# Phase 2's first product by Strassen's algorithm in a packed attention and two-mixer kernel

## The chip, the core and the metric

One core of a Trainium2 chip runs the whole program. TensorE multiplies, VectorE and ScalarE do the element-wise work, GpSimd a few memory sets, and SyncE issues the DMAs. The metric is the device time of one launch in microseconds (us). The kernel before took 1606.13 us, the median of three runs (1604.97 to 1606.46).

## The reference, cut to what matters

```python
x = attention_twice(q, k, v, p)          # 8 x 576 x 512
x = r * ((relu(xk @ w_k) ** 2) @ w_v)    # first mixer, "phase 1"
xt = x.transpose(0, 2, 1)
u = x + (xt @ U @ V).transpose(0, 2, 1)  # rank 32, over the sequence
out = u + relu(u @ w_ch1) @ w_ch2        # 512 -> 2048 -> 512, "phase 2"
```

The change concerns `u @ w_ch1`, the first product of phase 2: 4608 tokens by 512 by 2048.

## The kernel before

Attention and the first mixer run in 12 chunks of 384 tokens, one after another; four blocks of attention lie between the first of them. This is phase 1. Its result x goes to DRAM (x2_d), summed into a 64-row product with U (psu). Phase 2 takes the same 12 chunks again.

Every fp32 number that a large matmul reads is split into two fp32r tiles, hi (a copy) and lo (the number less hi), and a product is three matmuls: hi by hi, hi by lo, lo by hi (PASS). `split` makes hi on ScalarE or VectorE and lo on VectorE.

In phase 2 a chunk goes like this. `load_u` brings x back. `h_block` adds the U-V term, two matmuls of 512 columns into a bank called psh. `t_block` transposes u by four matmuls (pst) and splits the transpose into ut. For each of the 16 blocks m of 128 hidden units, `c1_block` accumulates 12 matmuls with w_ch1's block as the weights and 384 tokens as the moving columns, and forms the hidden block: relu on ScalarE is hi, and one VectorE operation is lo. `c2_block` then runs 9 matmuls of 512 columns with hid as weights and w_ch2 as moving operand, into three banks that stay open over all 16 blocks. Both products write banks that the profile names psc. `fin` adds u and sends the rows out. All of w_ch1 and w_ch2 is split once, in the first chunk of phase 2, and stays in SBUF.

The order of instructions is a planner's. Operations are written down in program order with the tiles that they read and write; `emit` (a list scheduler) walks simulated time and gives each engine the ready operation of the lowest class, on TensorE and SyncE then the earliest in program order, on the others the one that has been ready longest. It carries its own costs, and the engines run the order that results. Lower classes go first; the casts of phase 2's weights have class 3 and fall into gaps of phase 1. A tile of a pool is granted again only when all users of the one that it replaces are done, and tiles of one tag are granted in program order. All DMAs are issued by SyncE (L311).

PSUM has eight banks: three hold the second products (ps_v), two the first products (ps_k), one psu, two the rest (ps_a).

Of the kernel before, what the change touches and what calls it, by code (L numbers as in the profile page):

```python
# [100 lines left out]
class Plan:  # L101
# [202 lines left out]
            return self.size(o) + 100.0  # L304
        return self.add((eng,), fn, (), (out,))

    def dma(self, out, in_, cls=None, after=()):
        def fn():
            o = out.get() if isinstance(out, Ref) else out
            i = in_.get() if isinstance(in_, Ref) else in_  # L310
            self.nc.sync.dma_start(out=o, in_=i)  # L311
            runs = []
            for ap in (o, i):
                n, dims = 4, list(ap.ap)
                while dims and dims[-1][0] * 4 == n:
# [3 lines left out]
        return self.add(("sp",), fn, [in_] if isinstance(in_, Ref) else [],  # L319
                        [out] if isinstance(out, Ref) else [], cls=cls, after=after)  # L320


    LAT = {"pe": {"act": 197.0, "dve": 197.0, "pool": 224.0},
# [9 lines left out]
    def emit(self):  # L333
# [67 lines left out]
        while True:  # L401
# [46 lines left out]
            if e == "sp":  # L448
# [21 lines left out]
def packed_attention_moe_mixer_kernel(  # L470
# [20 lines left out]
    P = 128  # L491
# [29 lines left out]
    def dtile(name, shape, parts=(0,)):  # L521
        return plan.fixed(dram.tile(shape, F32, name=name), parts)
# [3 lines left out]
    xu_d = [dtile(f"xu_d{b}", [P, DM]) for b in range(NBP)]  # L526
    v_d = dtile("v_d", [NP, S])
    w1_d = [dtile(f"w1_d{m}", [P, NJ * P]) for m in range(MC)]
    w2_d = [dtile(f"w2_d{m}", [P, DM]) for m in range(MC)]

    def ctile(name, shape, dt=F32):
# [377 lines left out]
    for j in range(NJ):  # L909
        cast_rows(wk[j][0], w_k[j * P:(j + 1) * P, 0:512])  # L910

    es_c = ExitStack()
    hid_p, kk_p, r_p, x2_p, xs_p = cpools = [Pool(bufs=n) for n in (2, 3, 3, 3, 1)]

    def open_c():
        es_st.close()
        w1b.obj = open_pool(es_c, "w1b", 1, "left")
        for n, pl in zip("hid kk r x2 xs".split(), cpools):
            pl.obj = open_pool(es_c, n, pl.bufs, "left")

# [132 lines left out]
    order.append(("v", MK - 2))  # L1053


    es_2r, es_2l = ExitStack(), ExitStack()
    vx_p, st_p, w2r_p, ur_p, utr_p = rpools = [Pool(bufs=n) for n in (1, 3, 1, 1, 1)]
    NR = 2

    def open_r():  # L1060
        es_att.close()
        for n, pl in zip("vx st2 w2r ur utr".split(), rpools):
            pl.obj = open_pool(es_2r, n, pl.bufs, "right")

    w2l_p, ul_p, utl_p, h_p, o_p, stl_p = lpools = [Pool(bufs=n) for n in (1, 1, 1, 3, 2, 2)]

    def open_l():
        es_c.close()
        es_x.close()
        es_w1.close()  # L1070
        for n, pl in zip("w2l ul utl h o stl".split(), lpools):
            pl.obj = open_pool(es_2l, n, pl.bufs, "left")

    w2, u_t, ut_t, xt, hh = {}, {}, {}, {}, {}
    vst_ = []

    def make_v():
        vst = plan.tile(vx_p, [P, 2, NI, 2, 64], F32R, "vst", parts=(0, 1))
        vst_.append(vst)
        for c in range(2):  # L1080
# [3 lines left out]
            for i0, i1 in ((0, 5), (5, NI)):  # L1084
# [7 lines left out]
                sl = slice(c * 32, (c + 1) * 32)  # L1092
                split(vst.at(0)[:, 0, i0:i1, :, sl], vst.at(1)[:, 1, i0:i1, :, sl], sv)

    def load_w2(m):
        pl = w2r_p if m < NR else w2l_p
        a = plan.tile(pl, [P, 2, NJ, P], F32R, f"w1_{m}", parts=(0, 1))
        b = plan.tile(pl, [P, 2, DM], F32R, f"w2_{m}", parts=(0, 1))
        sa = plan.tile(st_p, [P, 512], F32, "s", name="s_2")
        plan.dma(sa[:, 0:512], w1_d[m])  # L1100
        split(half(a, 0), half(a, 1), sa[:, 0:512].rearrange("p (j c) -> p j c", j=NJ))
        sb = plan.tile(st_p if m < NR else stl_p, [P, 512], F32, "s", name="s_2")
        plan.dma(sb[:, 0:512], w2_d[m])
        split(half(b, 0), half(b, 1), sb[:, 0:512])
        w2[m] = (a, b)

    def load_xu(b):
        xa = plan.tile(st_p, [P, 512], F32, "s", parts=(0, 1), name="xa")
# [7 lines left out]
        plan.tt(X[64:128, :], xa[64:128, 0:512], X[64:128, :], sub)  # L1116
        xt[b] = X

    def load_u(n):
        b, c = chunks[n]  # L1120
        pl = (ur_p, ul_p)[n % 2]
        t = plan.tile(pl, [P, 3, DM], F32, "u", parts=(0, 1, 2))
        for i in range(3):
            ii = 3 * c + i
            plan.dma(t.at(i)[:, i, :], x2_d[b].at(ii)[:, ii * DM:(ii + 1) * DM])
        u_t[n] = t

    def h_block(n, t):
        b, c = chunks[n]
        if t == 0:  # L1130
            ut_t[n] = plan.tile((utr_p, utl_p)[n % 2], [P, 2, NJ, CW], F32R, "ut", parts=(0, 1))
        ps = plan.bank(ps_a, "psh")
        for a in range(2):
            plan.mm(ps, vst_[0].at(a)[:, a, 3 * c + t].rearrange("p b c -> p (b c)"), xt[b],
                    start=(a == 0), stop=(a == 1))
        u = u_t[n].at(t)[:, t, :]
        plan.tt(u, ps, u, add)

    def t_block(n, t):
        ps = plan.bank(ps_a, "pst")  # L1140
        for j in range(NJ):
            plan.transpose(ps[:, j * P:(j + 1) * P], u_t[n].at(t)[:, t, j * P:(j + 1) * P], ident)
        pv = ps.rearrange("p (j c) -> p j c", j=NJ)
        sl = slice(t * P, (t + 1) * P)
        ut = ut_t[n]
# [3 lines left out]
    def c1_block(n, m):  # L1149
        ps = plan.bank(ps_k, "psc1")  # L1150
        ut, w = ut_t[n], w2[m][0]
        i = 0
        for j in range(NJ):
# [3 lines left out]
        t = plan.tile(h_p, [P, 2, CW], F32R, "h", parts=(0, 1), name="hid")  # L1157
        plan.act(half(t, 0), ps[:, 0:CW], AF.Relu)
        plan.stt(half(t, 1), ps[:, 0:CW], 0.0, half(t, 0), ALU.max, sub)
        hh[n, m] = t  # L1160

    def c2_block(n, m):
        if m == 0:
            vps[:] = [plan.bank(ps_v, "psc2") for _ in range(3)]
        h, w = hh.pop((n, m)), w2[m][1]
        for t in range(3):
            for i, (a, wi) in enumerate(PASS):
                plan.mm(vps[t], half(h, a)[:, t * P:(t + 1) * P], half(w, wi),
                        start=(m == 0 and i == 0), stop=(m == MC - 1 and i == 2))

    def fin(n, t):
        b, c = chunks[n]
        o = plan.tile(o_p, [P, 512], F32, "o")
        plan.tt(o, vps[t], u_t[n].at(t)[:, t, :], add)
        dst = out[2 * b:2 * b + 2].rearrange("b (p i) f -> (b p) i f", i=NI)
        plan.dma(dst[:, 3 * c + t, :], o)

    casts = []
    for c in range(2):
# [22 lines left out]
    for n in range(len(chunks)):  # L1202
# [15 lines left out]
            load_x(n + 1)  # L1218
        for kind, m in order:
            if kind == "k":  # L1220
                if n + 1 == len(chunks) and m >= 1 and prep0:
# [18 lines left out]
        if b == NBP - 1 and c == 1:  # L1240
            make_v()
            for m in range(NR):
                load_w2(m)
            load_xu(0)
            load_u(0)
            prep0 = [f for t in range(3) for f in (lambda t=t: h_block(0, t), lambda t=t: t_block(0, t))]
    for t, x2 in enumerate(finish(len(chunks) - 1)):
        xu_block(len(chunks) - 1, t, x2)
    plan.open(lpools, cpools + xpools + [w1a, w1b], open_l, after=[opened_r])


    for n in range(len(chunks)):
        prep = []
        if n + 1 < len(chunks):
            b1, c1 = chunks[n + 1]
            load_u(n + 1)
            prep = [("h", 0), ("h", 1), ("t", 0), ("h", 2), ("t", 1), ("t", 2)]
            if c1 == 0:
                prep = [("x", b1)] + prep
        for m in range(MC + 2):  # L1260
            if m < MC:
                if m not in w2:
                    load_w2(m)
                c1_block(n, m)
            if m >= 2:
                c2_block(n, m - 2)
            if m >= 6 and prep:
                kind, a = prep.pop(0)
                if kind == "x":
                    load_xu(a)  # L1270
                elif kind == "h":
                    h_block(n + 1, a)
                else:
                    t_block(n + 1, a)
        for t in range(3):
            fin(n, t)
    plan.emit()
    es_2l.close()
    es_2r.close()


# [29 lines left out]
```

## Time and profile before

| What | us |
|---|---|
| median of three runs | 1606.13 |
| the profiled execution | 1604.61 |
| its span, first to last instruction | 1602.8 |
| TensorE busy in it | 1545.7 |
| VectorE busy | 762.7 |
| ScalarE busy | 599.0 |
| GpSimd busy | 3.1 |

A span of 1602.8 us lies 1.8 us inside the execution's time. Busy times of TensorE are those of pipelined instructions with modelled ends, so the mean time of one matmul in the profile is longer than the distance from one to the next; the distance is read from the starts in the timeline. TensorE's weight loads (PEld) lie beside its matmuls.

### The profile page before, as it was taken

The page shows a single profiled execution, that of the slowest core. Times are in us where ns is not written, and L with a number is a line of the kernel's source. Part 1 is how long each engine was busy: PE and PEld are TensorE (multiplying, and loading weights), DVE is VectorE, ACT ScalarE, POOL GpSimd, SP SyncE. Part 2 cuts the span into 40 slices and gives each one's busy share as a digit, 9 for nine tenths or more (in the row PEclk, how much of TensorE's full clock was granted, in tenths as well). Part 3 has the DMA queues.
Part 4 walks back from the last instruction along what each step waited for, and adds up shares of the span by engine and source line. Part 5 has one row for each costly group of instructions (what it writes and reads, how often), then busy time and mean ns, then how long its engine had stood idle before and what let it go on. Part 6 is the DMA issues. An engine that isn't in the chain of part 4 may idle for free.

```text
span 1602.8 us, 20779 instructions
## 1 busy us (share of the span) xinstructions
PE 1545.7 (96%) x8116; PEld 1348.5 (84%) x8116; DVE 762.7 (48%) x1627; ACT 599.0 (37%) x1293; POOL 3.1 (0%) x18
## 2 busy tenths in 40 slices
PE   6678799999999999999999999999999999999998
PEld 5557578888888888888899999899999989999997
DVE  4898868888887786443732221222122222221211
ACT  4676566676766665454421111111111111111110
POOL 0000000000000000000000000000000000000000
PEclk9888999999999999999999999999999999999999
DMA  9966446457634334100611101011010101101000
GB/s 186 226 171 160 119 111 172 122 166 195 157 120 140 138 123 128 53 3 18 212 39 33 40 1 40 1 47 40 1 40 1 40 1 40 40 1 40 0 21 20
DMA packets 146082, 128.51 MB, mean 80 GB/s; under 512 B 92736, under 2 KB 111488, under 8 KB 145984
## 3 DMA queue, kind: packets, MB, share of 16 engines
q1 hardware_dynamic: 145984, 127.18, 28.1%
q8 instruction: 64, 1.05, 0.3%
q14 instruction: 34, 0.28, 0.1%
HBM read 89.33 MB, written 37.82 MB: 79 GB/s over the span
## 4 chain that ended last, share of the span: by engine, by line
PE 91%; DMA 2%; ACT 2%; SPq 2%; DVE 2%; issue 0%; ACTq 0%; DVEq 0%
PE psc L197 50%; PE psv L197 12%; PE psk L197 12%; PE psr L197 6%; PE psat L197 4%; PE psat L208 2%; SPq L311 2%; PE psu L197 1%; PE psh L197 1%; PE pst L208 1%; ACT a L229 1%; DMA st<-in_moe_w_v_dram 1%; DMA st<-in_moe_w_k_dram 1%; DMA qin<-in_q_dram 0%; DVE m L250 0%
## 5 line engine op out<-in xcount | busy, mean ns | idle before, releaser
L197 PE MATMUL psc<-ut,w 128*128 128x384 f32 x2304 | 433.6, 337 | 0.0
L197 PE MATMUL psc<-w,hid 128*128 128x512 f32 x1728 | 426.1, 393 | 1.1 <-ACT hid L229 1.1
L197 PEld LDWEIGHTS psc<-ut,w 128*128 128x128 f32 x2304 | 405.5, 188 | 11.7
L197 PEld LDWEIGHTS psc<-w,hid 128*128 128x128 f32 x1728 | 321.7, 188 | 61.1 <-ACT hid L229 1.5
L265 DVE SCALAR_TENSOR_TENSOR hid<-psc,hid 128x384 fp32r<-128x384 f32 x192 | 107.1, 558 | 466.9 <-ACT hid L229 466.8
L229 ACT ACTIVATE hid<-psc 128x384 fp32r<-128x384 f32 x192 | 94.3, 492 | 610.7 <-PE psc L197 610.7
L197 PE MATMUL psk<-xk,wk 128*128 128x384 f32 x1152 | 232.3, 343 | 0.5 <-DVE xk L250 0.4
L197 PE MATMUL psv<-wv,kk 128*128 128x512 f32 x864 | 227.4, 401 | 4.0 <-ACT wv L280 2.9
L197 PEld LDWEIGHTS psk<-xk,wk 128*128 128x128 f32 x1152 | 202.0, 189 | 12.6 <-issue 3.9
L197 PEld LDWEIGHTS psv<-wv,kk 128*128 128x128 f32 x864 | 159.2, 189 | 37.5 <-ACT wv L280 3.8
L197 PE MATMUL psr<-wr,xr 128*128 128x512 f32 x432 | 114.7, 408 | 3.4 <-ACT xr L280 3.4
L197 PEld LDWEIGHTS psr<-wr,xr 128*128 128x128 f32 x432 | 81.0, 194 | 23.7 <-ACT xr L280 4.1
L250 DVE TENSOR_TENSOR kk<-sq,kk 128x384 fp32r<-128x384 f32 x96 | 52.7, 554 | 60.8 <-ACT kk L280 60.4
L229 ACT ACTIVATE sq<-psk 128x384 f32<-128x384 f32 x96 | 46.7, 489 | 83.9 <-PE psk L197 83.4
L229 ACT ACTIVATE m<-x,om_t 128x384 f32<-128x384 f32 x96 | 57.6, 611 | 10.8 <-DVE xk L250 5.8
L262 DVE SCALAR_TENSOR_TENSOR m<-x,mu_t,m 128x384 f32<-128x384 f32 x96 | 57.9, 612 | 1.7 <-ACT m L229 1.5
L250 DVE TENSOR_TENSOR ut<-pst,ut 128x512 fp32r<-128x512 f32 x36 | 24.9, 692 | 68.3 <-ACT ut L229 68.3
L250 DVE TENSOR_TENSOR u<-psh,u 128x512 f32<-128x512 f32 x36 | 24.9, 692 | 49.5 <-PE psh L197 48.4
L229 ACT ACTIVATE ut<-pst 128x512 fp32r<-128x512 f32 x36 | 21.5, 599 | 67.9 <-PE pst L208 67.9
L250 DVE TENSOR_TENSOR o<-psc,u 128x512 f32<-128x512 f32 x36 | 24.6, 688 | 46.1 <-PE psc L197 44.7
L280 ACT ACTIVATE kk<-sq 128x384 fp32r<-128x384 f32 x86 | 44.7, 522 | 3.0 <-DVE sq L296 1.0
L229 ACT ACTIVATE a<-st 128x512 f32<-128x512 f32 (+2 forms) x55 | 35.6, 657 | 19.2 <-DMA st<-in_moe_w_ch_dram 4.7
(125 smaller groups left out, 1361.2 us busy)
## 6 DMA issues: line engine op xcount, KB each, us to landing
st<-in_moe_w_ch_dram SPq DMA_DIRECT2D x32, 512.0 KB, 4.4
qin<-in_q_dram SPq DMA_DIRECT2D x32, 288.0 KB, 5.5
x_d<-xo SPq DMA_DIRECT2D x16, 576.0 KB, 3.4
x_d<-x SPq DMA_DIRECT2D x36, 256.0 KB, 2.9
u<-x_d SPq DMA_DIRECT2D x36, 256.0 KB, 3.4
out_dram<-o SPq DMA_DIRECT2D x36, 256.0 KB, 2.0
kin<-in_k_dram SPq DMA_DIRECT2D x32, 256.0 KB, 5.8
vin<-in_v_dram SPq DMA_DIRECT2D x32, 256.0 KB, 5.1
```

The source lines that it names most:

```text
L197: self.nc.tensor.matmul(o, l, r, start=start, stop=stop, **k)
L208: self.nc.tensor.transpose(out.get(), in_.get(), ident.get())
L229: self.nc.scalar.activation(o, in_.get(), func, **k)
L250: return self.elem(engs, lambda e, o, x, y: e.tensor_tensor(out=o, in0=x, in1=y, op=op), out, [a, b], self.TT, cls)
L262: ("dve",), lambda e, o, x, y, z: e.scalar_tensor_tensor(out=o, in0=x, scalar=z, in1=y, op0=op0, op1=op1), out, [a, b, s], {"dve": (1.042, ...
L265: ("dve",), lambda e, o, x, y: e.scalar_tensor_tensor(out=o, in0=x, scalar=s, in1=y, op0=op0, op1=op1), out, [a, b], self.TT, cls)
L280: self.nc.scalar.activation(o, i, AF.Copy)
L311: self.nc.sync.dma_start(out=o, in_=i)
```

## The change

Phase 2 takes 9 groups of 512 tokens instead of 12 chunks of 384. For each pair of hidden blocks (f, 8 of them) the 512 x 256 weights and the 512 tokens are cut in two by two blocks: 256 of the model dimension by 128 hidden units, and 256 by 256 tokens. The four results of 128 x 256 come from seven block products with combined operands (the Winograd form of Strassen's algorithm), where eight would be the plain way. A block product is 2 x 3 matmuls of 128x128 weights and 256 columns.

The combined weights are formed by VectorE in the last two chunks of phase 1 (`make_ws`, class 3), split, and written to DRAM by SyncE; in phase 2 each block product loads its own 256 KB again (`load_ws`), issued by GpSimd's queue into one of 12 tiles. The combined tokens (`operands`) are formed for the next group behind the seventh of the eight steps of the one before. Three banks a, b and c collect the products; ScalarE and VectorE read them between products to form the shared sums. The second product's matmuls are the same, in another order; three of its four parts of a step run in the next step (`late`). Its results now take four banks, the first product three, and h_block and t_block share one.

```diff
-    def dma(self, out, in_, cls=None, after=()):
+    def dma(self, out, in_, cls=None, after=(), eng="sp"):
-            self.nc.sync.dma_start(out=o, in_=i)
+            (self.nc.sync if eng == "sp" else self.nc.gpsimd).dma_start(out=o, in_=i)
-                clock[e] = t + 60.0
+                clock[e] = t + (60.0 if e == "sp" else 1000.0)
...
+    vx_p, st_p, u_p, wb_p = rpools = [Pool(bufs=n) for n in (1, 5, 9, 12)]
...
+    def make_ws(f):
+        r = []
+        for m in (2 * f, 2 * f + 1):
+            t = plan.tile(st_p, [P, 512], F32, "s", name="raw_1")
+            plan.dma(t, w1_d[m])
+            r.append(t)
+        a11, a12, a21, a22 = [t[:, h * 256:(h + 1) * 256] for t in r for h in range(2)]
+        bl = [plan.tile(wb_p, [P, 2, 256], F32R, "wb", parts=(0, 1)) for _ in range(7)]
...
+        plan.tt(s1, a21, a22, add)
+        plan.tt(s2, s1, a11, sub)
+        plan.tt(s3, a11, a21, sub)
+        plan.tt(s4, a12, s2, sub)
+        for i, src in enumerate((a11, s2, s1, a12, s3, s4, a22)):
+            split(half(bl[i], 0), half(bl[i], 1), src)
+        for i in range(7):
+            plan.dma(ws_d[f].at(i)[:, i * 512:(i + 1) * 512], bl[i].rearrange("p a c -> p (a c)").bitcast(F32))
+
+    def load_ws(f, i):
+        t = plan.tile(wb_p, [P, 2, 256], F32R, "wb", parts=(0, 1))
+        plan.dma(t.rearrange("p a c -> p (a c)"), ws_d[f].at(i)[:, i * 512:(i + 1) * 512], eng="pool")
+        return t
...
-        plan.act(ut.at(0)[:, 0, :, sl], pv, AF.Copy)
-        plan.tt(ut.at(1)[:, 1, :, sl], pv, ut.at(0)[:, 0, :, sl], sub)
+        plan.copy(ut_[q].at((t // 2, 2 + t // 2))[:, :, t * P:(t + 1) * P], ps.rearrange("p (j c) -> p j c", j=NJ))
+
+    def operands(q):
...
+        t1, t2 = [kc(plan.tile(st_p, [P, 512], F32, "s", name="sums")) for _ in range(2)]
+        o11 = whole(b11)
+        plan.tt(t1, b12, b11, sub)
+        plan.tt(t2, b22, t1, sub)
+        plan.tt(b11, b21, t2, sub)
+        plan.tt(b12, b22, b12, sub)
+        ops[q] = [o11] + [whole(x) for x in (t2, t1, b21, b12, b22, b11)]
+
+    def product(q, f, i, name, fresh):
+        if fresh:
+            bank_abc[name] = plan.bank(ps_c1, "psc1")
+        ps = bank_abc[name][:, 0:256]
+        w, x = load_ws(f, i), ops[q][i]
+        n = 0
+        for k in range(2):
             for wi, a in PASS:
-                plan.mm(ps[:, 0:CW], w.at(wi)[:, wi, j, :], ut.at(a)[:, a, j, :], start=(i == 0), stop=(i == 11))
-                i += 1
+                plan.mm(ps, half(w, wi)[:, k * P:(k + 1) * P],
+                        half(x, a)[:, k * 256:(k + 1) * 256],
+                        start=(fresh and n == 0), stop=(n == 5), skip_group_check=True)
+                n += 1
+        return ps
...
+            a = product(q, f, 0, "a", True)
+            p1 = tmp_tile()
+            plan.copy(p1, a, ("act",))
+            b = product(q, f, 1, "b", True)
+            s = tmp_tile()
+            plan.tt(s, p1, b, add)
+            if late:
+                late.pop("22")()
+            c = product(q, f, 2, "c", True)
+            p5 = tmp_tile()
+            plan.copy(p5, c, ("act",))
+            if late:
+                late.pop("21")()
+            product(q, f, 3, "a", False)
+            h11 = hidden(a)
+            if late:
+                late.pop("12")()
+            product(q, f, 4, "b", False)
+            x22 = tmp_tile()
+            plan.tt(x22, p1, b, add)
+            plan.tt(x22, x22, p5, add)
+            h22 = hidden(x22)
+            product(q, f, 5, "c", False)
+            plan.tt(s, s, c, add)
+            h12 = hidden(s)
+            c2_block(q, 2 * f, 0, h11, False)
+            product(q, f, 6, "b", False)
+            plan.tt(p1, p1, b, add)
+            h21 = hidden(p1)
+            end = f == NF - 1
+            late = {"22": lambda q=q, f=f, h=h22: c2_block(q, 2 * f + 1, 1, h, False),
+                    "21": lambda q=q, f=f, h=h21, end=end: c2_block(q, 2 * f + 1, 0, h, end),
+                    "12": lambda q=q, f=f, h=h12, end=end: c2_block(q, 2 * f, 1, h, end)}
```

## Rows read from the trace of the kernel before

**Rows 1.** Windows: the stretch, its length; busy us and instructions by engine; clock, DMA, GB/s

```profile
600.00:763.50 163.50, 163.50 (x808) 145.71 (x807) 80.51 (x160) 79.35 (x155) 0.71 (x2) 1.00 0.15 50
763.50:1597.50 834.00, 832.89 (x4237) 753.45 (x4235) 202.51 (x340) 129.66 (x252) 0.00 (x0) 1.00 0.10 32
...
763.50:803.50 40.00, 38.93 (x200) 35.32 (x199) 28.65 (x51) 17.16 (x32) 0.00 (x0) 1.00 0.69 218
```

**Rows 2.** The chain that ended last, by engine and by line

```profile
PE 91%; DMA 2%; ACT 2%; SPq 2%; DVE 2%; issue 0%; ACTq 0%; DVEq 0%
PE psc L197 50%; PE psv L197 12%; PE psk L197 12%; PE psr L197 6%; PE psat L197 4%; PE psat L208 2%; SPq L311 2%; PE psu L197 1%; PE psh L197 1%; PE pst L208 1%; ACT a L229 1%; DMA st<-in_moe_w_v_dram 1%; DMA st<-in_moe_w_k_dram 1%; DMA qin<-in_q_dram 0%; DVE m L250 0%
```

**Rows 3.** Groups by line and form, phase 2: busy us, mean ns, idle before

```profile
L197 PE MATMUL psc<-ut,w 128*128 128x384 f32 x2304 | 433.6, 337 | 0.0
L197 PE MATMUL psc<-w,hid 128*128 128x512 f32 x1728 | 426.1, 393 | 1.1 <-ACT hid L229 1.1
L197 PEld LDWEIGHTS psc<-ut,w 128*128 128x128 f32 x2303 | 405.3, 188 | 11.7
...
L265 DVE SCALAR_TENSOR_TENSOR hid<-psc,hid 128x384 fp32r<-128x384 f32 x192 | 107.1, 558 | 466.9 <-ACT hid L229 466.8
L229 ACT ACTIVATE hid<-psc 128x384 fp32r<-128x384 f32 x192 | 94.3, 492 | 610.7 <-PE psc L197 610.7
```

**Rows 4.** Timeline of TensorE in one step of phase 2: start, us, what

```profile
1004.39 0.62 PE L197 MATMUL psh<-X,vst 128*128 128x512 f32 x2
1004.85 2.27 PE L197 MATMUL psc<-ut,w 128*128 128x384 f32 x12
1006.95 2.24 PE L197 MATMUL psc<-w,hid 128*128 128x512 f32 x9
1009.03 0.60 PE L208 MATMUL pst<-ident,u 128*128 128x128 f32 x4
1009.39 2.33 PE L197 MATMUL psc<-ut,w 128*128 128x384 f32 x12
```

**Rows 5.** Timelines of TensorE at matmuls of 256 columns, and of a weight load

```profile
346.15 0.38 PE L197 MATMUL psat<-th,ppz 64*128 64x256 f32 x1
346.37 0.28 PE L197 MATMUL psat<-tl,ppz 64*128 64x256 f32 x1
346.49 0.27 PE L197 MATMUL psat<-th,ppz 64*128 64x256 f32 x1
...
346.26 0.19 PEld L197 LDWEIGHTS psat<-tl,ppz 64*128 64x128 f32 x1
```

**Rows 6.** SyncE's DMAs at the seam; the same loads to landing; first and last

```profile
772.66 19.12 SPq L311 DMA_DIRECT2D s<-w_d  x19
...
s<-w_d SPq DMA_DIRECT2D x32, 256.0 KB, 3.1
...
L311 SPq DMA_DIRECT2D w_d<-m x32: 319/327/1530, 248.8 to 595.2; - x32
```

**Rows 7.** Groups by line and form: the nearest to the new operations

```profile
L280 ACT ACTIVATE xo<-psat 128x256 f32<-128x256 f32 x22 | 7.8, 386 | 8.4 <-PE psat L197 8.4
...
L250 DVE TENSOR_TENSOR vst<-s_v,vst 128x256 fp32r<-128x256 f32 x2 | 0.8, 422 | 0.0
...
L250 DVE TENSOR_TENSOR m<-m,a 128x512 f32<-128x512 f32 x52 | 35.1, 683 | 0.1
...
L280 ACT ACTIVATE w<-s 128x512 fp32r<-128x512 f32 x23 | 14.4, 630 | 11.3 <-DMA s<-w_d 11.1
L283 DVE CAST w<-s 128x512 fp32r<-128x512 f32 x9 | 3.6, 423 | 1.7 <-DMA s<-w_d 1.7
```

**Rows 8.** Timeline of TensorE at the seam: start, us, what, idle before

```profile
771.26 1.42 PE L197 MATMUL psc<-w,hid 128*128 128x512 f32 x5 [1.07 <-ACT hid L229]
```

**Rows 9.** Timeline of the tail

```profile
1596.14 1.37 DVE L250 TENSOR_TENSOR o<-psc,u 128x512 f32<-128x512 f32 x2 [3.72 <-PE psc L197]
...
1599.01 0.69 DVE L250 TENSOR_TENSOR o<-psc,u 128x512 f32<-128x512 f32 x1 [1.49 <-DMA out_dram<-o]
```

More of the change, by code (lines that the diff above doesn't have):

```diff
@@ L1117, in load_xu @@
         xt[b] = X
[L1119 to L1129, printed above, removed]
-        if t == 0:
[L1131 to L1137, printed above, removed]
@@ L1162, in c2_block, with load_u @@
[L1162 to L1166, printed above, removed]
-            for i, (a, wi) in enumerate(PASS):
[L1168 to L1176, printed above, removed]
+    def load_u(T):
+        b, i = divmod(T, NI)
+        u_t[T] = plan.tile(u_p, [P, DM], F32, "u")
+        plan.dma(u_t[T], x2_d[b].at(i)[:, i * DM:(i + 1) * DM])
@@ new lines, in packed_attention_moe_mixer_kernel, with h_block, t_block @@
+    prep_banks = [ps_a]
+    def h_block(T):
+        b, i = divmod(T, NI)
+        ps = plan.bank(prep_banks[0], "psh")
+        for a in range(2):
+            plan.mm(ps, vst_[0].at(a)[:, a, i].rearrange("p b c -> p (b c)"), xt[b], start=(a == 0), stop=(a == 1))
+        plan.tt(u_t[T], ps, u_t[T], add)
+    def t_block(T):
+        q, t = divmod(T, 4)
+        if t == 0:
+            ut_[q] = plan.tile(xin_p, [P, NJ, 4 * P], F32, "x", parts=(0, 1, 2, 3), name="ut")
+        ps = plan.bank(prep_banks[0], "pst")
+        for j in range(NJ):
+            plan.transpose(ps[:, j * P:(j + 1) * P], u_t[T][:, j * P:(j + 1) * P], ident)
+        plan.copy(ut_[q].at((t // 2, 2 + t // 2))[:, :, t * P:(t + 1) * P], ps.rearrange("p (j c) -> p j c", j=NJ))
@@ new lines, in hidden, with c2_block @@
+    def hidden(src):
+        t = plan.tile(mix_p, [P, 2, CW], F32R, "mx", parts=(0, 1), name="hid")
+        hi, lo = [half(t, i)[:, 0:256] for i in range(2)]
+        plan.act(hi, src, AF.Relu)
+        plan.stt(lo, src, 0.0, hi, ALU.max, sub)
+        return t
+    def c2_block(q, m, th, h, last):
+        if (q, th) not in first:
+            first.add((q, th))
+            acc[q, th] = [plan.bank(ps_c2, "psc2") for _ in range(2)]
+            fresh = True
+        else:
+            fresh = False
+        w = w2[m]
+        for t in range(2):
+            for i, (a, wi) in enumerate(PASS):
+                plan.mm(acc[q, th][t], half(h, a)[:, t * P:(t + 1) * P], half(w, wi),
+                        start=(fresh and i == 0), stop=(last and i == 2))
+        if last:
+            for t in range(2):
+                T = 4 * q + 2 * th + t
+                b, i = divmod(T, NI)
+                u = u_t.pop(T)
+                plan.tt(u, acc[q, th][t], u, add)
+                dst = out[2 * b:2 * b + 2].rearrange("b (p i) f -> (b p) i f", i=NI)
+                plan.dma(dst[:, i, :], u)
@@ L1239, in packed_attention_moe_mixer_kernel @@
                 opened_r = plan.open(rpools, A0.pools + cv.pools, open_r)
-        if b == NBP - 1 and c == 1:
-            make_v()
-            for m in range(NR):
+        if n > NCAST:
+            plan.cls = 3
+            for f in range(NF // 2):
+                make_ws((n - NCAST - 1) * (NF // 2) + f)
+            plan.cls = 1
+        if n == NCAST + 1:
+            make_v()
+            load_xu(0)
+            for T in range(4):
+                load_u(T)
+            prep0 = [f for T in range(4) for f in (lambda T=T: h_block(T), lambda T=T: t_block(T))]
@@ L1243, in packed_attention_moe_mixer_kernel @@
+        if n == NCAST + 2:
+            operands(0)
+            for m in range(2):
                 load_w2(m)
-            load_xu(0)
-            load_u(0)
-            prep0 = [f for t in range(3) for f in (lambda t=t: h_block(0, t), lambda t=t: t_block(0, t))]
     for t, x2 in enumerate(finish(len(chunks) - 1)):
         xu_block(len(chunks) - 1, t, x2)
-    plan.open(lpools, cpools + xpools + [w1a, w1b], open_l, after=[opened_r])
-    for n in range(len(chunks)):
-        prep = []
[L1254 to L1276, printed above, removed]
@@ new lines, in packed_attention_moe_mixer_kernel @@
+    plan.open(lpools, cpools, open_l, after=[opened_r])
+    ps_c2, ps_c1 = banks[0:3] + banks[5:6], banks[3:5] + banks[6:7]
+    prep_banks[0] = banks[7:8]
+    late = {}
+    for q in range(NQ):
+        prep = []
+        if q + 1 < NQ:
+            T0 = 4 * q + 4
+            for T in range(T0, T0 + 4):
+                load_u(T)
+            hs = [[lambda T=T: h_block(T)] for T in range(T0, T0 + 4)]
+            for T in range(T0, T0 + 4):
+                if T % NI == 0:
+                    hs[T - T0].insert(0, lambda T=T: load_xu(T // NI))
+            ts_ = [[lambda T=T: t_block(T)] for T in range(T0, T0 + 4)]
+            prep = [[], hs[0], hs[1] + ts_[0], hs[2] + ts_[1], hs[3] + ts_[2], ts_[3], [lambda q=q: operands(q + 1)]]
+        for f in range(NF):
+            if q == 0:
+                for m in (2 * f + 2, 2 * f + 3):
+                    if m < MC:
+                        load_w2(m)
+            a = product(q, f, 0, "a", True)
[31 more added lines that the diff above has]
+                    "12": lambda q=q, f=f, h=h12, end=end: c2_block(q, 2 * f, 1, h, end)}
+            if prep:
+                for g in prep.pop(0):
+                    g()
@@ L1277, in packed_attention_moe_mixer_kernel @@
+    for x in ("22", "21", "12"):
+        late.pop(x)()
     plan.emit()
```

84 lines of the change are left out of this document (47 added, 37 removed).

## The prediction

> **What bounds the kernel now.** I read the stages first [rows 1]. Phase 2, the stretch that the change rewrites, is 763.5 to 1597.5 us, 834 us long, and TensorE is busy in 832.9 of them at a granted clock of 1.00, its 2.4 GHz level. VectorE has work in 202.5 us of it, ScalarE in 129.7, GpSimd in none, and the DMA engines 10%. The chain of waits says the same: 91% of it is TensorE, and half of the span is the two products of phase 2, both under the name psc [rows 2]. So phase 2 is as long as its matmuls, if nothing else gets in. The means of the groups [rows 3] are latencies of overlapping instructions and no pitch; the pitch comes from the starts in the timeline [rows 4]. Twelve matmuls of the first product begin at 1004.85 and the next group at 1006.95: 2.10 us, 0.175 us each. Nine of the second product take 2.08 us, 0.231 each; a pair of U-V matmuls (psh) 0.46, four transposes (pst) 0.36. With the counts of rows 3, 192 x (2.10 + 2.08) + 33 x (0.46 + 0.36) = 829.6 us, which leaves 4.4 for the seam and small change: the pitches carry the stage.
>
> **The change: matmuls.** The first product goes from 2304 matmuls of 384 columns to 9 groups x 8 steps x 7 block products x 6 = 3024 of 256 columns: 7/8 of the columns, but 720 more instructions, each with its own weight load. The second product keeps 72 x 24 = 1728 matmuls of 512, and there are again 36 psh pairs and 36 transpose groups. All hangs on the pitch at 256 columns. The two pitches of rows 4 lie on a line of 0.4375 ns a column with 7 ns over; at 256 it gives 0.119 us. The trace has such a row nearly: fp32r matmuls of 256 columns, weights of 64 rows, each with a load of its own, start 0.12 us apart [rows 5]. I take 0.119. The ends: 0.112 if only the columns counted (256 x 0.4375 ns); and 0.188, the length of a weight load's record, if loads did not overlap [rows 3]. Against the latter, in rows 5 a load of 0.19 us begins 0.11 after the matmul before it, and the matmul that needs it 0.11 later, before the record ends.
> Before: 2304 x 0.175 = 403.2 us. After: 3024 x 0.119 = 359.9. The term is -43.3 us (-64.5 at 0.112; +165 at 0.188; it is zero at 0.133).
> A rule of the Trainium skill stands against the trace here. TensorE: Matmul & The Clock Gate, section Back-to-back issue gap, gives N/2.4 + 2.5 ns at full clock. By it 256 columns cost 109 ns and the 3024 cost an estimated 330 us, 73 us less than what the trace has for the old ones. But the same rule gives 162.5 and 216 ns where rows 4 have 175 and 231; the measurement decides.
>
> **Loads of the combined weights.** GpSimd's queue now issues 9 x 8 x 7 = 504 loads of 256 KB. TensorE's time of phase 2 after the change is about 359.9 + 1728 x 0.231 + 33 x 0.82 = 786 us, so one load is due every 1.56 us; they cost nothing if they come at that pace, since 12 tiles let the queue run some 19 us ahead and nothing else is queued on GpSimd there (its busy time in the stretch is zero [rows 1]). The trace has no transfer of this queue and none that goes from fp32 into an fp32r tile, so its pace is bounded: below, SyncE's queue issued 19 loads of the same size and 2 KB rows in 19.12 us at the seam, 1.01 us a load [rows 6]; above, if a load began only when the one before had landed, 3.1 us [rows 6]. The break-even, where loads alone fill the old 834 us, is 1.65. I take the lower end, as it is a sustained rate of this very size, and cost the loads at nothing. Were the cover gone, 0.1 us over 1.56 costs 50 us in all. Outputs and u loads add 18.9 MB, some 24 GB/s to the stream's 168; 40 us at the seam moved 218 [rows 1].
>
> **VectorE and ScalarE.** A step (two hidden blocks, 512 tokens) runs 42 x 0.119 + 24 x 0.231 = 10.5 us on TensorE. It has 6 ScalarE operations on 128x256 (two copies, four relus), 0.386 us by the nearest row, and 9 on VectorE, 0.422 [rows 7]: 2.3 and 3.8 us. That is more than today (192 x (0.49 + 0.56) [rows 3] over the phase), but under 40% of a step. What can bite is the chain inside it, since three banks are written twice or thrice. With a product at 0.71 and a half of the second product at 1.39: product 3 ends 5.6 into the step, relu, subtraction and three hand-overs of some 0.2 give the hidden block at 7.0, and its user starts at 8.4. Product 4 ends at 7.7, VectorE has read its bank by 8.5, and product 6 wants it at 9.8. Each slack is 1.3 us or more, three VectorE operations long. I cost it at nothing.
> Once a group, the 7 operands of the next are formed in the last step: 4 + 7 operations of 0.68 on VectorE and 7 copies of 0.63 on ScalarE or 0.42 on VectorE [rows 7], 7.5 us more in 10.5 that hold 3.8 already, plus what is left of adds and copies. Only three of ten tiles are free early; the rest wait for the old group's last products. The first products of the next group need the first operands only. I give each of the 8 seams 0.4 us, 3 in all.
>
> **Before phase 2.** The combined weights are formed during the last two chunks: 8 x (4 + 7) VectorE operations of 0.422 [rows 7] = 37 us, 56 copies of 0.39 on ScalarE, and the first operands, 7.5. From 600 to 763.5 us VectorE is free for 83 us and ScalarE for 84 [rows 1]; the last of the DRAM weights that they read was written at 595.2 and can be read from there on [rows 6]. TensorE is busy in all of that stretch, and the new work has the lowest class, so it goes into gaps. On SyncE's queue 56 writes (256 KB, 14.7 MB) come in front of what follows, beside the 50 GB/s of that stretch; the 14 first-product loads and splits that stood after 763.5 go away. What is late next is the seam itself: the last transpose of the first group now stands in the last k block, some 8 us ahead of phase 2, and product 1 needs two subtractions and a split after it. Today the seam has one wait of 1.07 us [rows 8]; I take 3 more.
>
> **Tail.** Today the last addition waits 1.49 us for an output buffer and comes after the two before it [rows 9]; now two additions are made in place, and the end has bubbles of a few tenths in its last hidden block. Zero in sum.
>
> **Sum.** -43.3 + 3 + 3 = -37 us. The profiled execution took 1604.6 us (span 1602.8); the median of the runs is 1.5 above. 1604.6 - 37 is 1567.3, and 1568 or 1569 on the median's footing; I say 1568.
>
> **Rivals.**
> *A. The loads set the pace.* Place: GpSimd's queue, with TensorE waiting at the weight load of each block product. It decides from 1.56 us a load, and the kernel is slower than before from 1.65. At 2.05, midway between the two ends of rows 6, the loads alone last 1033 us and the kernel ends near 763.5 + 1033 + 8 = 1805. For it: no row shows this queue, and a 256 KB load is short next to its 3.1 us of landing, so it needs two in flight at all times. Against: 12 tiles, an idle engine, and SyncE's 1.01. The Trainium skill, DMA: Bandwidth & Descriptors, section Bandwidth, has for loads issued by GpSimd 0.95 us at 64 KB and 6.15 at 1 MB; a straight line between these is an estimated 1.99 us at 256 KB, and 504 of them would end the kernel near 1775. SyncE's 1.01 for the same bytes speaks against it, no run yet shows it for GpSimd.
> *B. Waits inside the steps eat the gain.* Banks a, b and c are read by ScalarE and VectorE between products; if VectorE is late by 1.9 us somewhere in each step, past the 1.3 of slack, 0.6 x 72 = 43 us are gone and the time is about 1605; a step that loses 1 us makes it 1635. For it: adds, operands and outputs share VectorE with the chain, and each is 0.68 long. Against: under half of VectorE is used, and TensorE's order can move on to the next product.
> *C. Weight loads don't hide under 256 columns.* Decides at 0.133 us; at 0.188, 1604.6 + 165 + 6 = 1776. Rows 5 speak against it, with 64 rows of weights though, not 128.
>
> **Chances.** The forecast 0.67, A 0.15, B 0.14, C 0.04. The forecast's own range is 1540 (0.112 a matmul, no waits) to 1595 (0.125, 15 us of waits). The range goes on to 1640, over B and the near edge of A. A change under 0.2%, 3 us, can't be told from none. Faster: the forecast and 0.05 of A and B at their mild ends, 0.72; within 0.2%: 0.05, from B; slower: 0.23.
>
> **What would show it.** Right: a phase 2 near 795 us with TensorE busy throughout, groups of six 256-column matmuls every 0.71 us, idle time before them under 1%. A would show as gaps before the weight loads, released by a DMA, and loads from GpSimd more than 1.6 us apart; B as gaps released by VectorE or ScalarE; C as groups of six over 0.8 us with no gap between groups. A seam past 770 us would show that the combined weights came late.

## The result, and the profile after

The changed kernel takes 1570.7 us (median of 4 runs, 1566.98 to 1570.89), the kernel before 1605.7 on the same chip: ratio 0.9777, 95% interval 0.976 to 0.9794. The prediction was 1568, in a range of 1540 to 1640. The profiled execution took 1570.7 us with a span of 1568.9, 33.9 less than the 1602.8 of before.

The stages first, as in [rows 1]: windows of the change, with length, busy us and instructions by engine (PE, PEld, DVE, ACT, POOL), clock, DMA share, GB/s.

```profile
600.00:764.00 164.00, 164.00 (x815) 146.47 (x815) 114.60 (x265) 99.77 (x211) 8.56 (x16) 1.00 0.57 190
764.00:1563.50 799.50, 795.21 (x4959) 715.89 (x4958) 377.24 (x843) 217.99 (x529) 259.77 (x492) 1.00 0.70 189
763.50:779.50 16.00, 13.00 (x71) 9.97 (x69) 13.23 (x24) 7.74 (x15) 3.17 (x6) 1.00 0.96 301
779.50:786.50 7.00, 5.71 (x24) 5.21 (x25) 5.83 (x12) 3.22 (x7) 1.05 (x2) 0.51 0.43 134
786.50:1563.50 777.00, 777.00 (x4868) 701.13 (x4867) 358.68 (x810) 207.52 (x508) 255.56 (x484) 1.00 0.70 187
```

Phase 2 went from 834 us [rows 1] to about 800. From 786.5 us on TensorE is busy in 777.00 of 777.00 us at the 2.4 GHz level, while the DMA engines are busy in 70% of the time. All that phase 2 waits for lies in its first 23 us: 16.00 - 13.00 and 7.00 - 5.71 make 4.29 us of idle, where [rows 8] have one wait of 1.07; and in the second of these windows the granted clock is 0.51, the 1.2 GHz level, after TensorE had stood in several gaps. Before phase 2 VectorE took on 34 us and ScalarE 20 more than in [rows 1] (80.51, 79.35), and TensorE stayed busy throughout.

The groups of phase 2 in the changed kernel, as in [rows 3]: busy us, mean ns of one, idle before and what ended it.

```profile
L197 PE MATMUL psc<-w,hid 128*128 128x512 f32 x1728 | 445.9, 393 | 0.0
L197 PEld LDWEIGHTS psc<-ob,wb 128*128 128x128 f32 x3024 | 407.9, 191 | 26.4
L197 PE MATMUL psc<-ob,wb 128*128 128x256 f32 x3024 | 421.0, 284 | 0.0
L311 POOL DMA_DIRECT2D wb<-ws_d x504 | 266.4, 529 | 610.6 <-PE psc L197 513.1
L250 DVE TENSOR_TENSOR tmp<-tmp,psc 128x256 f32<-128x256 f32 x288 | 120.7, 419 | 151.3 <-PE psc L197 142.4
L229 ACT ACTIVATE hid<-tmp 128x256 fp32r<-128x256 f32 x216 | 85.2, 417 | 255.6 <-DVE tmp L250 255.5
L280 ACT ACTIVATE tmp<-psc 128x256 f32<-128x256 f32 x144 | 54.5, 379 | 136.0 <-PE psc L197 136.0
```

The matmul of 256 columns records 284 ns, but that is its latency; the price is in the starts. The steady part of phase 2, timeline of TensorE: start, us, what.

```profile
1202.59 1.55 PE L197 MATMUL psc<-w,hid 128*128 128x512 f32 x6
1203.98 0.88 PE L197 MATMUL psc<-ob,wb 128*128 128x256 f32 x6
1204.69 1.55 PE L197 MATMUL psc<-w,hid 128*128 128x512 f32 x6
1206.08 0.88 PE L197 MATMUL psc<-ob,wb 128*128 128x256 f32 x6
1206.79 1.55 PE L197 MATMUL psc<-w,hid 128*128 128x512 f32 x6
1208.18 1.59 PE L197 MATMUL psc<-ob,wb 128*128 128x256 f32 x12
```

Six of 256 columns take 0.71 us (1204.69 - 1203.98), the number that the prediction asked to see, and six of 512 take 1.39, as it reckoned for half of a second product. The rows of the GpSimd queue say the rest. In the groups above its 610.6 us of idle end with a matmul (513.1 of them): it waits until TensorE frees a tile. The waits from 790 to 1560 us (engine, line, waited for: us, times, longest us) say so too:

```profile
POOL wb L311 <- PE psc L197: 467.0, 326, 4.2
```

The loads are ahead: in that window no wait of TensorE or of its weight loads ends with a DMA. In the DMA view their median way to landing is 3.1 us, and the queues' packets hold the engines as follows (packets, MB, share of 16 engines' span):

```profile
q0 software_dynamic: 72576, 132.15, 32.4%
q1 hardware_dynamic: 154048, 141.87, 31.2%
...
wb<-ws_d POOLq DMA_DIRECT2D x504, 256.0 KB, 3.1
```

**The account.** For each matmul I took the distance from its start to the next start and summed these by kind, so that waits count with the matmul ahead of them. "Prep" is psu, psh and pst, the U-V products and the transposes that prepare a group; "rest" is all before and between, "end" what follows the last matmul's start. The experiments stand below the two kernels.

```
us                first   second   prep    rest    end     span
before            405.9   398.4    50.9    741.9   5.7     1602.8
the change        364.2   398.9    57.1    743.8   5.0     1568.9
the change again  364.1   398.9    56.6    743.4   5.0     1568.0
e1_eighth         415.7   398.9    57.3    745.1   5.0     1622.0
e2_two_loads      532.5   505.5    69.5    744.9   4.8     1857.1
e3_no_stream      364.0   399.3    55.8    744.9   5.0     1568.9
e4_sync_queue     364.2   399.0    59.0    741.8   4.5     1568.6
e5_hold3          365.5   399.5    59.0    745.5   4.4     1573.8
e6_hold6          386.9   402.0    59.5    740.7   4.4     1593.5
e7_late_w2        364.8   398.9    54.4    744.3   5.0     1567.4
e8_low_w2         364.5   399.2    54.8    745.7   5.0     1569.2
e9_few_tiles      366.6   417.5    63.8    742.2   4.7     1594.8
e10_paced_w2      363.7   399.3    54.4    744.4   5.0     1566.9
e12_two_sync      373.4   403.7    56.3    743.4   4.3     1580.9
```

The 33.9 us are -41.7 (first product), +0.5 (second), +6.2 (prep, 5.7 of it at the seam into phase 2), +1.9 (rest) and -0.7 (end). The first product has a share in the seam too: its matmuls in the first two steps of phase 2 take 132.5 and 145.8 ns from start to start, those of every later step 118.7 to 121.2, and that makes 1.7 us. "Rest" goes from 740.7 to 745.7 over kernels that run nearly the same code there, so its +1.9 is scatter of single executions.

### The profile page after: what moved, and what is told of

It reads as the page before. It is cut to its first block, busy times and chain, and to the rows that moved or that the text cites. A ratio compares the mean times of both kernels' runs of the same rounds, so it can differ in the third digit from the quotient of the medians.

```text
span 1568.9 us, 24697 instructions
## 1 busy us (share of the span) xinstructions
PE 1511.3 (96%) x8836; PEld 1313.2 (84%) x8836; DVE 971.1 (62%) x2231; ACT 706.4 (45%) x1623; POOL 270.2 (17%) x522
## 3 DMA queue, kind: packets, MB, share of 16 engines
q1 hardware_dynamic: 154048, 141.87, 31.2%
## 4 chain that ended last, share of the span: by engine, by line
PE 90%; DMA 3%; DVE 3%; ACT 2%; SPq 1%; issue 0%; DVEq 0%; ACTq 0%
PE psc L197 48%; PE psv L197 12%; PE psk L197 12%; PE psr L197 6%; PE psat L197 5%; PE psat L208 3%; SPq L311 1%; PE psh L197 1%; PE psu L197 1%; PE pst L208 1%; DMA st<-in_moe_w_k_dram 1%; DMA st<-in_moe_w_v_dram 1%; ACT a L229 1%; DMA qin<-in_q_dram 1%; DVE m L250 0%
## 5 line engine op out<-in xcount | busy, mean ns | idle before, releaser
L197 PE MATMUL psc<-w,hid 128*128 128x512 f32 x1728 | 445.9, 393 | 0.0
L197 PEld LDWEIGHTS psc<-ob,wb 128*128 128x128 f32 x3024 | 407.9, 191 | 26.4
L197 PE MATMUL psc<-ob,wb 128*128 128x256 f32 x3024 | 421.0, 284 | 0.0
L311 POOL DMA_DIRECT2D wb<-ws_d x504 | 266.4, 529 | 610.6 <-PE psc L197 513.1
L250 DVE TENSOR_TENSOR tmp<-tmp,psc 128x256 f32<-128x256 f32 x288 | 120.7, 419 | 151.3 <-PE psc L197 142.4
L229 ACT ACTIVATE hid<-tmp 128x256 fp32r<-128x256 f32 x216 | 85.2, 417 | 255.6 <-DVE tmp L250 255.5
L265 DVE SCALAR_TENSOR_TENSOR hid<-psc,hid 128x256 fp32r<-128x256 f32 x72 | 30.5, 424 | 189.5 <-ACT hid L229 189.5
L280 ACT ACTIVATE tmp<-psc 128x256 f32<-128x256 f32 x144 | 54.5, 379 | 136.0 <-PE psc L197 136.0
L265 DVE SCALAR_TENSOR_TENSOR hid<-tmp,hid 128x256 fp32r<-128x256 f32 x216 | 86.2, 422 | 20.5 <-ACT hid L229 14.9
L250 DVE TENSOR_TENSOR kk<-sq,kk 128x384 fp32r<-128x384 f32 x96 | 52.7, 554 | 44.0 <-ACT kk L280 43.3
L229 ACT ACTIVATE hid<-psc 128x256 fp32r<-128x256 f32 x72 | 27.5, 382 | 105.1 <-PE psc L197 105.1
```

The lines of the kernel that those rows point to most:

```text
L197: self.nc.tensor.matmul(o, l, r, start=start, stop=stop, **k)
L229: self.nc.scalar.activation(o, in_.get(), func, **k)
L250: return self.elem(engs, lambda e, o, x, y: e.tensor_tensor(out=o, in0=x, in1=y, op=op), out, [a, b], self.TT, cls)
L265: ("dve",), lambda e, o, x, y: e.scalar_tensor_tensor(out=o, in0=x, scalar=s, in1=y, op0=op0, op1=op1), out, [a, b], self.TT, cls)
L280: self.nc.scalar.activation(o, i, AF.Copy)
L311: (self.nc.sync if eng == "sp" else self.nc.gpsimd).dma_start(out=o, in_=i)
```

## Experiments

My theory after the result: phase 2 is the sum of its matmul pitches, the stream costs nothing, the slack of the banks is wide enough, and the only loss is the seam. Of e1, e2, e5, e6 and e12 there is one execution each.

**An eighth product (e1_eighth).** The last block product's six matmuls run twice, with the same weights, tokens and load: 432 more in all, and another result.

```diff
-        for k in range(2):
+        for k in (0, 1, 0, 1) if i == 6 else (0, 1):
...
```

> The changed kernel with an eighth block product in each step: the six matmuls of the seventh are run twice with the same weights and tokens, so the result is another. Theory (TensorE's matmuls set the pace, 0.120 us each): 432 more matmuls cost 51.8 us, 1619 to 1626, more than the kernel before: eight products of 256 columns would lose, and the gain is the seventh eighth. Rival (the loads set the pace, or waits inside the steps): the new matmuls fit into time that is idle anyway, 1571 to 1590.

1623.8 us in one run, beside 1605.6 for the kernel before. Windows, columns as above:

```profile
764.00:1617.00 853.00, 848.73 (x5399) 768.86 (x5397) 379.90 (x846) 219.25 (x532) 259.77 (x492) 1.00 0.67 177
```

The first product grew by 415.7 - 364.2 = 51.5 us, 0.119 a matmul. Each matmul left out is worth its pitch, and eight products of 256 columns would be slower than the kernel before: the gain is the missing eighth alone, less what 720 more instructions cost.

**No stream (e3_no_stream).** The seven combined weights of the first step are loaded once and kept, and every step multiplies with them, so the result is another.

```diff
...
+        if i in kept:
+            return kept[i]
...
+        kept[i] = t
```

> The changed kernel, but each of the seven combined weights is loaded once and kept: 497 of the 504 loads are left out, and all steps multiply with the weights of the first, so the result is another. Theory: the loads cost TensorE nothing once phase 2 runs, the stretch after the seam stays within 3 us of 779.5, and the seam gains at most its 4 to 6 us since the DMA engines are free for the w_ch2 loads: 1564 to 1571. Rival: the stream slows TensorE's reads; the 256-column matmuls fall from 0.1205 to the 0.115 of the quickest tenth and the 512-column ones from 0.2318 to 0.229, 17 + 5 us, 1549.

1568.2 (1565.75 to 1570.73), ratio 0.9763 [0.9746, 0.9779], which overlaps that of the change. Its window has the DMA engines at 7%, GpSimd at nothing, and TensorE as before:

```profile
784.00:1563.50 779.50, 778.81 (x4874) 702.68 (x4873) 360.11 (x812) 207.37 (x508) 0.00 (x0) 1.00 0.07 23
```

The first product takes 364.0 us without the stream and 364.2 with it. That the stream, at this pace, slows TensorE's reads is refuted.

**SyncE issues the loads (e4_sync_queue).**

```diff
-        plan.dma(t.rearrange("p a c -> p (a c)"), ws_d[f].at(i)[:, i * 512:(i + 1) * 512], eng="pool")
+        plan.dma(t.rearrange("p a c -> p (a c)").bitcast(F32), ws_d[f].at(i)[:, i * 512:(i + 1) * 512])
```

> The changed kernel with the 504 loads issued by SyncE's queue instead of GpSimd's (the tile is addressed as fp32). Theory: a load due every 1.55 us fits either queue, and what counts is TensorE: 1566 to 1576. Rival: on SyncE's queue a load that waits for a free tile holds up the u loads and the outputs behind it, and the next group's operands come late: over 1580.

1571.1 (1568.04 to 1571.95), ratio 0.9782 [0.9768, 0.9797]: the same. At one load in 1.56 us the queue doesn't matter.

**Twice the stream, by GpSimd (e2_two_loads) and by SyncE (e12_two_sync).** Each load is issued twice, into two of the twelve tiles; for SyncE with the line of e4.

```diff
-        t = plan.tile(wb_p, [P, 2, 256], F32R, "wb", parts=(0, 1))
-        plan.dma(t.rearrange("p a c -> p (a c)"), ws_d[f].at(i)[:, i * 512:(i + 1) * 512], eng="pool")
+        for _ in range(2):
+            t = plan.tile(wb_p, [P, 2, 256], F32R, "wb", parts=(0, 1))
+            plan.dma(t.rearrange("p a c -> p (a c)"), ws_d[f].at(i)[:, i * 512:(i + 1) * 512], eng="pool")
```

> The changed kernel with each load of a combined weight issued twice, into two of the 12 tiles, of which one is used: 1008 loads, one due every 0.78 us. It measures the pace of GpSimd's queue, on which the rival of slow loads rested. Theory: the transfers bound it at no better than SyncE's 1.01 us a load seen before, so 1018 us of loads and 1780 us or more (at 1.2 us a load 1980). Rival: only the issue on GpSimd counts, 0.53 us and 0.19 between two, 0.72 in all; then the loads still fit and the time stays within 10 us of 1571.

> Each load issued twice, as in the run before that took 1.08 us a load through GpSimd's queue, now by SyncE's queue (the tile addressed as fp32). Theory: the limit is the DMA engines' time for the 2 KB rows, 99 ns median on GpSimd's queue and 84 on SyncE's in the runs so far, so the loads go at 0.92 us and the kernel ends near 764 + 925 + 5 = 1694. Rival: the limit is memory or the whole of the engines whatever the queue, 1830 to 1870.

GpSimd: 1859.2 us. SyncE: 1582.8, far under both of its expectations. Of the first the window of phase 2, a line of its waits, then its queues and loads; columns as above:

```profile
784.00:1852.00 1068.00, 900.78 (x4883) 737.98 (x4883) 374.12 (x820) 214.96 (x507) 514.78 (x973) 0.94 0.93 256
```

```profile
PE psc L197 <- DMA wb<-ws_d: 124.2, 155, 3.2
```

```profile
q0 software_dynamic: 145152, 264.31, 52.3%
...
wb<-ws_d POOLq DMA_DIRECT2D x1008, 256.0 KB, 4.1
```

The same two of the second:

```profile
784.00:1576.00 792.00, 784.95 (x4870) 700.11 (x4870) 360.52 (x808) 219.06 (x513) 0.00 (x0) 1.00 0.99 349
```

```profile
q1 hardware_dynamic: 299200, 406.17, 78.4%
...
wb<-ws_d SPq DMA_DIRECT2D x1008, 256.0 KB, 5.0
```

From GpSimd 973 loads took 1068 us, 1.10 us each, with the DMA engines busy in 93% of it: this is rival A at work. TensorE stands for 1068 - 901 = 167 us, mostly until a load has landed, and the clock falls to a mean of 0.94, so part of the waits is paid a second time in slower matmuls. GpSimd's queue waits for TensorE to free a tile only 4.9 us in all from 800 to 1850 us, so it isn't the number of tiles that holds it. From SyncE the 1008 loads fit between 764 and 1576 us (some 0.81 each), at 349 GB/s. No wait of TensorE ends with one of them there, so 0.81 is not the limit of that queue, which no run shows; SyncE's 1.01 at the seam [rows 6] was none either. The 12 us over the change lie between TensorE's matmuls, in waits for hidden blocks among others: with twice the loads to place, the planner wrote another order. Engine time per packet: the 145152 packets of GpSimd's queue take 0.523 x 16 x 1857.1 us, 0.107 us each; SyncE's loads take what its queue has over the change's, (0.784 x 1580.9 - 0.312 x 1568.9) x 16 us for 299200 - 154048 packets, 0.083 each. At the single pace the two are nearer: 0.112 in the change and, worked out in the same way, 0.097 in e4. Why the same bytes hold the engines 1.15 to 1.3 times as long from GpSimd's queue isn't settled: fp32 goes into an fp32r tile there, and was passed as fp32 on SyncE, so queue and type changed together.

**A longer way through the banks (e5_hold3, e6_hold6).** One VectorE addition behind product 4 runs four times, or seven; each is 0.42 us.

```diff
-            plan.tt(x22, p1, b, add)
+            for _ in range(4):
+                plan.tt(x22, p1, b, add)
```

> The changed kernel with the addition that reads bank b after the fifth product run four times instead of once (same result): the bank is held 1.26 us longer in each step, and VectorE has 1.26 us more work. Theory: the slack is 1.3 us or more, so 0 to 15 us more, 1571 to 1586. Rival (the steps are already on the edge): 72 x 1.0 us or more, over 1640.

> The same with the addition run seven times: bank b is held 2.52 us longer. Theory: 1.2 us over the slack in each step, 87 us, unless the planner moves other work into the gap: 1600 to 1660. If the slack was much larger than predicted, under 1590.

Three more (1.26 us): 1575.6. Six more (2.5 us): 1595.3, below its expectation. Its window, and from its waits the two lines that matter:

```profile
784.00:1588.50 804.50, 789.16 (x4866) 706.36 (x4865) 516.34 (x1246) 202.04 (x500) 255.50 (x484) 0.99 0.68 180
```

```profile
POOL wb L311 <- PE psc L197: 474.8, 281, 5.7
...
PEld psc L197 <- DVE tmp L250: 17.6, 17, 4.1
```

By the account, first product, second and prep grew by 3.8 us (365.5 + 399.5 + 59.0 against 820.2) and by 28.2. So with 1.26 us more a step loses 0.05 us, and with 2.5 us more 28.2/72 = 0.39 us, not the 1.2 that 2.5 less 1.3 would make. But the planner knew of the additions and wrote TensorE's order anew around them (in e4 and e11 the order in phase 2 is that of the change, in e5 and e6 it isn't). That fits a slack of 1.3 us and doesn't measure it: what a VectorE that is late without the planner's knowledge would cost, no run shows.

**Four tiles for twelve (e9_few_tiles).**

```diff
-    vx_p, st_p, u_p, wb_p = rpools = [Pool(bufs=n) for n in (1, 5, 9, 12)]
+    vx_p, st_p, u_p, wb_p = rpools = [Pool(bufs=n) for n in (1, 5, 9, 4)]
```

> The changed kernel with 4 tiles for the streamed weights instead of 12. Theory: four tiles run some 3 x 1.56 = 4.7 us ahead, a load needs 3.1 us to land and some 0.7 for its issue, so most loads still come in time, 1571 to 1590. Rival: landings stretch to 5 us and more under load, and TensorE waits at each, over 1600. With 12 tiles the question does not arise: 17 us ahead.

1597.4 (1592.51 to 1599.71), ratio 0.9946 [0.9929, 0.9963]: worse than expected. Window and waits from 784 us on:

```profile
784.00:1592.00 808.00, 789.51 (x4886) 703.84 (x4886) 363.95 (x813) 214.73 (x521) 260.81 (x494) 1.00 0.71 184
```

```profile
PEld psc L197 <- DMA wb<-ws_d: 21.1, 21, 2.5
...
PE psc L197 <- DMA wb<-ws_d: 14.9, 17, 2.1
```

With four tiles three quarters of the gain are gone with the same loads from the same queue: 18.5 us idle in this window, and weight loads that wait for a landing. Here too the planner, which knows the tiles, wrote another order, and the account can't part what that cost. A queue that is fast enough on the average is not enough; in the change the loads are free because they are far ahead.

**The seam.** This is the chain of waits there in the changed kernel (start, us, what; pieces of under 0.05 us left out):

```profile
772.15 5.24 DMA s<-w_d
777.42 0.63 ACT w L280
778.04 0.49 ACT ut L280
778.58 0.75 PE psh L197 x2
779.36 0.70 DVE u L250
780.10 1.13 PE pst L208 x4
781.26 0.61 ACT ut L280
781.91 0.79 PE psh L197
782.70 3.84 PE psc L197 x18
```

A load of second-product weights takes 5.24 us among its like (the engines are at 96%, 301 GB/s), its split stands on ScalarE ahead of a copy of the next group's transposes, and TensorE's order has that group's preparation ahead of the seventh product. Three ways to loosen this: let the planner count 3 us more for these loads, so that other work comes first (e7_late_w2); give loads and splits the lowest class (e8_low_w2); or issue them two a step, behind product 0, with the 3 us of e7 as well (e10_paced_w2). The change itself ran again beside the last (e11_change).

```diff
...
-                op.fin = wire + 1700.0
+                op.fin = wire + 1700.0 + op.extra
...
-        plan.dma(sb[:, 0:512], w2_d[m])
+        plan.dma(sb[:, 0:512], w2_d[m]).extra = 3000.0
```

```diff
+                plan.cls = 2
...
+                plan.cls = 1
```

```diff
...
+            a = product(q, f, 0, "a", True)
...
-                        load_w2(m)
-            a = product(q, f, 0, "a", True)
+                        load_w2(m, [plan.ops[-1]])
```

> The changed kernel with one number of the planner: it counts 3 us more for the landing of each w_ch2 load at the start of phase 2, so that the splits of these loads stand later in ScalarE's and VectorE's order. Theory: the 4.3 us that TensorE idles between 773 and 783 us, and the lower clock behind it, come from splits that wait for a late load (5.2 us to landing) in front of the transposes' copies and the sixth operand; with the splits later the idle time goes below 1.5 us and the time falls by 4 to 7 us, to 1564 to 1567. Rival: the seam is held by the sheer VectorE work of the operands (7.5 us); then the order of the splits changes nothing, 1570 to 1572.

> The changed kernel with the w_ch2 loads and splits of phase 2's first group in class 2 instead of 1, so that they go behind all other ready work; the planner's landing times stay. Theory (late splits block the queues): part of the gain only, since the planner still believes that the loads land early, 1565 to 1570. Rival (operand work): 1570 to 1572.

> The changed kernel with the 14 w_ch2 loads of the first group paced: the pair for step f+1 is issued behind the first block product of step f, not all at the seam, and the planner counts 3 us more for their landing. Theory (at the seam late loads and their splits block VectorE's and ScalarE's queues, on which bank b waits): with one pair at a time the idle time of the seam falls from 4.3 us to under 1.5 and the low clock after it goes, 4 to 7 us less than the changed kernel beside it. Rival: the seam idles for the operands or for the U-V sums; no more than 1 us less.

> The changed kernel itself once more, beside the paced one on the same chip: 1567 to 1571 us.

Times: e7 1566.0 (1565.72 to 1569.22), ratio 0.9759 [0.9744, 0.9773]; e8 1568.3, 0.977 [0.9756, 0.9785]; e10 1568.7, 0.9772 [0.9758, 0.9785]; the change again, on e10's chip, 1570.4 (1569.09 to 1572.19), 0.9783 [0.977, 0.9797]. The windows of the seam in e7, e10 and the change again:

```profile
763.50:784.00 20.50, 17.52 (x95) 14.01 (x95) 16.52 (x31) 11.57 (x24) 3.86 (x8) 0.95 0.86 262
```

```profile
763.50:784.00 20.50, 17.91 (x97) 14.61 (x96) 14.76 (x28) 7.88 (x17) 3.69 (x7) 0.92 0.68 205
```

```profile
763.50:784.00 20.50, 16.76 (x86) 13.31 (x85) 17.03 (x32) 10.47 (x21) 3.18 (x7) 0.87 0.82 259
```

Idle falls from 20.50 - 16.76 = 3.74 us to 2.98 and 2.59, not under the 1.5 that I had expected, and prep from 56.6 to 54.4 in both (54.8 in e8). To see the whole seam, I took from the time between phase 2's first matmul and 787 us what its matmuls would need at the pitches of the later groups. Lost there are about 1.4 us before, 8.6 in the change, 8.1 in the change again, 6.5 in e7, 6.9 in e8 and 6.0 in e10, each in one execution. So the late loads are some 2 of the 7 us that the seam costs over before, not nearly all of it. The time of e7 lies in its expected range, then, but the reason given for it holds in part only. What is left shows in e10's timeline of TensorE:

```profile
776.85 0.73 PE L197 MATMUL psh<-X,vst 128*128 128x512 f32 x2 [0.40 <-ACT ut L280]
778.37 0.66 PE L208 MATMUL pst<-ident,u 128*128 128x128 f32 x4 [0.79 <-DVE u L250]
779.72 1.22 PE L197 MATMUL psh<-X,vst 128*128 128x512 f32 x2 [0.69 <-ACT ut L280]
```

It is the serial way from product to addition to transpose to copy in the next group's preparation, for which TensorE waits with the seventh product queued behind it. Another order there was not tried. The e7 version is the fastest measured (its profile is of the slowest of its four executions); its interval overlaps the change's, so I don't call it faster.

## Why the prediction was right

**The pitch at 256 columns: right, the term 1.6 us too large.** -43.3 was forecast, -41.7 measured: 0.1204 us (364.2/3024) for 0.119, and 0.1762 for the old 0.175 (405.9/2304). The difference is not in the pitch. Behind the seam a matmul of 256 columns takes 0.1199 us, 362.5 for all 3024; the 1.7 us above that are those of the first two steps. Each half of the term was some 2.7 us too small (403.2 for 405.9, 359.9 for 362.5), and luck lets the two cancel. The row nearest to the new matmuls [rows 5] was read kindly: it has two distances, 0.22 and 0.12, and the second was taken. Rival C, decided at 0.133, falls: the weight loads record 191 ns each and are hidden. By the rule of the Trainium skill, TensorE: Matmul & The Clock Gate, section Back-to-back issue gap, which gives it for a single matmul by itself and not for a stream with weight loads, the 256 columns would have cost 109 ns; the trace has 120, and the straight line through the two rows of before was the better guide.

**The second product: right.** Costed as unchanged; +0.5 us of 398.

**Loads at nothing: right, and for the reason given.** Without the stream the first product is no shorter. The pace itself, which no row of before had, is 1.10 us a load with the DMA engines busy in 93% of the time, close to SyncE's 1.01 [rows 6] and far from 3.1; A's point of 1.56 isn't reached. That 1.01 was taken for a bound from below, and e12 with 0.81 shows that it was none, which changes nothing here. Its mechanism is real: at twice the stream the kernel takes 1859 us. The straight line through the figures of the Trainium skill, DMA: Bandwidth & Descriptors, section Bandwidth, estimated 1.99 us a load; measured is little more than half of that. What the prediction passed over quickly is how much hangs on the twelve tiles: with four, 27 of the 35 us are lost, in another order of matmuls though.

**The slack in the banks at nothing: right; its size of 1.3 us not measured.** TensorE has no idle time from 786.5 us on, so rival B, which would have needed 0.6 us a step, falls. Three more additions cost 4 us in 72 steps, and 2.5 us more on VectorE 0.39 a step, with an order that the planner fitted to them. Its price was too high where the planner knows of the delay, as it took each microsecond past the slack for a microsecond lost. Its sums are some 5 us low: 43 and 72 us on 1568 are 1611 and 1640, not 1605 and 1635. And the additions in the chain last 0.42 us each, not 0.68.

**The seams: the sum nearly right by luck, both parts wrong.** 3 us were forecast for eight group seams and 3 for the seam into phase 2. The group seams cost nothing: TensorE has no idle time from 786.5 us on, and each group from the second to the eighth takes 87.95 us from its first matmul to that of the next, its last step at 119.2 to 119.4 ns a matmul. The seam into phase 2 cost some 7 over before (5.7 in prep, 1.7 in the first product): 3.2 of idle and some 3 from the 7 us at the 1.2 GHz level, in which 5.7 us of matmuls take about twice their time; the last 1 us I can't place. That the clock falls after a few short gaps, 4.3 us of idle in all, was not in the prediction. Its sign, a seam past 770 us because the combined weights come late, was wrong as to cause: late were second-product weights, and behind them the next group's preparation.

**Before phase 2 and the tail: right.** First matmul of phase 2 at 764.1 for 763.5, with 34 us more on VectorE in that stage where 44 were worked out; the end is 0.7 us shorter.

## What to carry to other kernels

Where TensorE is busy throughout, a change of algorithm is worth (matmuls) x (pitch at their width), and a straight line through two widths of the same trace gave the third to about 1%. A stream of operands that is needed at a known pace is free if it is due later than it can come and has enough tiles to run ahead. Test both: here twice the stream cost far more than the gain through GpSimd's queue and a third of it through SyncE's, and with a third of the tiles three quarters of the gain were lost. Look for the loss where the stages meet: there the order of the next stage's preparation, a crowded DMA and the clock add up.

## What the runs showed that I had not expected

- With the same 1008 loads of 256 KB the core's DMA moved 349 GB/s when SyncE issued them and 256 when GpSimd did, at 0.083 and 0.107 us of engine time a packet (queue and element type changed together).
- Waits of TensorE can be paid twice: with 167 us of idle in e2 the granted clock of phase 2 was 0.94, and the two products grew from 763 to 1038 us, waits included. With 18.5 us of idle in e9 the clock stayed at 1.00.
- The stages before phase 2 differ by 5 us between single executions of nearly the same code (740.7 to 745.7), while the first product repeats within 1.1 (363.7 to 364.8 in the change, e3, e4, e7, e8, e10 and e11). Differences of 1 to 2 us are better read from the stage than from the whole time.
